# Warm-up products of 512 columns in place of 128, in a fused attention and gated-MLP block

## The chip, the cores and the metric

The kernel runs on one core of one Trainium2 chip. The metric is device time in microseconds (us) of one execution. Several runs of a kernel are taken and their median is quoted with the lowest and the highest; one further execution is taken with the hardware profiler on, and all rows of the trace come from that one. The engines are named as the profile names them: PE (TensorE, matrix products; PEld is its loading of weights), DVE (VectorE), ACT (ScalarE), POOL (GpSimd) and SP (SyncE, which here only issues transfers).

## What is computed

The input x has 2048 tokens of 512 features in bf16. It is normalised, and two branches work on the result: attention with 32 heads of 16 features in a sliding window of 256 tokens, and a gated MLP whose gate mixes tokens with a 2048 x 2048 matrix. The output is the sum of x and both branches.

```python
xn = layernorm(x)                                   # 2048 x 512
# branch A
q, k, v = split(xn @ wqkv)                          # 32 heads of 16
p = softmax(mask(q @ k.T / 4))                      # 0 <= i - j < 256
A = (p @ v) @ wo
# branch B
z = gelu(xn @ w_in)                                 # 2048 x 1376
z1, z2 = z[:, :688], layernorm(z[:, 688:])
B = (z1 * (w_sp @ z2 + b_sp[:, None])) @ w_out
out = x + A + B
```

## The kernel before, in words

Tokens are cut into 16 blocks of 128, one partition per token of the block. The program is one long order written out by hand: three strings, STAGE1, STAGE2 and STAGE3 (lines 68 to 172), hold short commands such as `t,0,v`, and `run` (line 616) executes them one after another by a table of functions (line 607). No scheduler reorders anything; every engine works through its own instructions in the order of these strings, and waits where a tile that it needs isn't ready.

STAGE1 prepares x and computes gelu(xn @ w_in). For each block, `a` takes mean and variance on DVE (lines 263 to 266). The first three blocks go a quicker way than the others: `B` only subtracts the mean on DVE into xc (line 275), `t` transposes the block on PE in four products with the identity (line 284), `T` copies the transposed halves from PSUM into xcT on ACT (line 290), and the scale by 1/sqrt(variance) is applied later. The gate `z` multiplies a block by w_in (lines 304 to 315): per chunk of 128 features one product of 512 and one of 176 columns, four chunks, into one of three PSUM tiles, za, zb and zo. `y` applies gelu on ACT (line 322). From block 3 on the input is normalised in full before it is transposed. STAGE2 computes the projections, attention scores, exponentials and weighted sums together with the token mixing, and STAGE3 the last output projections.

Ahead of STAGE1 the function that holds the kernel issues the loads of x and w_in on the queues of SP and ACT (lines 666 to 677), lets POOL build the identity matrix `ident` (line 680), and calls `table(0)`, which makes ACT load its function table, and `warm(WARM)`. The function `warm(n)` (lines 647 to 651) issues n products on PE of the identity with the identity. Their results go into the PSUM tile zo and are never read; the gate of block 2, the first real writer of zo, overwrites them. WARM is 29 (line 33). The command `W,5` in the first line of STAGE1 (line 69) calls `warm` again with five, between the transposes of block 0 (`t,0,v`) and the copy of them (`T,0,v,A`):

```python
WARM = 29
...
a,0 B,0 a,1 t,0,v W,5 T,0,v,A B,1 A,0,2 z,0,1,a,0,1 t,1,w T,1,w,A a,2 z,0,1,a,1,2 z,1,1,b,0,1
```

So the order on PE at the start is: 29 warm-up products, four transposes of block 0, five warm-up products, the first half of the gate of block 0 (two chunks), four transposes of block 1, the second half of that gate, and so on.

## Time and profile before

| | us |
|---|---|
| median of 3 runs | 259.92 |
| lowest and highest | 258.59 and 260.62 |
| profiled execution, its own time | 258.91 |
| its span, first to last instruction | 257.1 |
| PE busy | 248.5 |
| DVE busy | 186.0 |
| ACT busy | 181.0 |
| POOL busy | 90.9 |

The span is the time between the first and the last instruction of the program on the core; the 1.8 us beside it lie around it. Busy times are of each engine by itself, and they overlap. In the rows below, a name such as L649 is a line of the kernel; `zo<-ident` means that the instruction reads ident and writes zo; `x29` is the number of instructions that a row gathers. The ends of products on PE are modelled, since products overlap in the array: the distance between two starts tells more than the duration of one.

### The profile page before, as it was taken

The numbers are of one execution on the slowest core, as the hardware profiler recorded it, in microseconds if no ns is written. First come the engines' busy times: TensorE is split into PE (matmuls) and PEld (weight loads), VectorE is DVE, ScalarE is ACT, GpSimd is POOL, SyncE is SP. The second block draws the span as 40 slices with busy tenths as digits, with TensorE's granted clock in tenths as the row PEclk, the third lists the DMA queues.
The fourth block names the chain that finished last, engine by engine and source line by source line (L and its number), as shares of the span: only waits on it lengthen the run. The fifth ranks groups of instructions, "written<-read, shape, count | busy, mean of one in ns | idle before, by whom it ended". The sixth has DMA issues, their size and how long they took to land. (4 is left out here: it accounts for less than half of the span.)

```text
span 257.1 us, 9010 instructions
## 1 busy us (share of the span) xinstructions
PE 248.5 (97%) x3880; PEld 137.1 (53%) x3916; DVE 186.0 (72%) x410; ACT 181.0 (70%) x142; POOL 90.9 (35%) x170
## 2 busy tenths in 40 slices
PE   7999999999999999999999999999999999999994
PEld 6565555433456555555555655655656544444541
DVE  4887877888797686778684776857877577667763
ACT  3686476899978687777868777776777786767400
POOL 7524110430015176017197055505545142511120
PEclk9999999999999999999999999999999999999999
DMA  7995743289404897749669476997755532764433
GB/s 237 362 247 98 118 82 83 61 134 234 96 3 95 102 145 144 129 98 170 116 122 165 105 101 118 123 161 128 156 123 96 94 74 84 112 128 116 115 102 102
DMA packets 69847, 32.65 MB, mean 127 GB/s; under 512 B 60800, under 2 KB 66912, under 8 KB 69808
## 3 DMA queue, kind: packets, MB, share of 16 engines
q1 hardware_dynamic: 64288, 21.19, 44.9%
q0 software_dynamic: 4576, 9.71, 17.6%
q10 hardware_dynamic: 944, 1.19, 1.3%
q8 instruction: 30, 0.49, 0.9%
q14 instruction: 9, 0.07, 0.1%
HBM read 8.41 MB, written 2.10 MB: 41 GB/s over the span
## 5 line engine op out<-in xcount | busy, mean ns | idle before, releaser
L443 ACT ACTIVATE E<-sS 128x2048 bf16<-128x2048 f32 x76 | 142.6, 1877 | 41.9 <-PE sS L429 40.8
L551 PE MATMUL w<-z,wspT 128*128 128x344 bf16 x512 | 92.6, 310 | 0.7 <-DVE z1u L558 0.2
L551 PEld LDWEIGHTS <-wspT 128*128 128x128 bf16 x512 | 46.9, 98 | 31.5 <-issue 5.9
L387 POOL DMA_DIRECT2D kbd<-kz x48 | 29.5, 622 | 59.8 <-DVE kz L379 57.7
L366 POOL DMA_DIRECT2D q<-qs x54 | 28.0, 527 | 30.5 <-DVE qs L355 23.1
L452 DVE TENSOR_TENSOR E<-E,mask 128x1024 bf16<-128x1024 bf16 x52 | 34.7, 676 | 4.3 <-ACT E L443 4.3
L339 PE MATMUL w<-xnT,wqkv 128*128 128x512 bf16 x106 | 35.7, 380 | 0.7 <-issue 0.3
L429 PE MATMUL sS<-q,kbd 32*128 32x320 bf16 (+4 forms) x816 | 30.4, 244 | 0.5 <-ACT E L443 0.2
L558 DVE SCALAR_TENSOR_TENSOR z1u<-w,b_all,z1u 128x344 bf16<-128x344 f32 x32 | 18.2, 568 | 16.3 <-PE w L551 16.2
L518 DVE STREAM_TRANSPOSE a<-oP 128x512 f32<-128x512 f32 x32 | 22.7, 709 | 4.7 <-PE oP L510 4.6
L309 PEld LDWEIGHTS <-xnT 128*128 128x128 bf16 x208 | 18.3, 98 | 12.4
L510 PE MATMUL oP<-E,v_all 64*17 64x256 bf16 (+3 forms) x1920 | 24.7, 230 | 0.0
L510 PEld LDWEIGHTS <-v_all 64*17 64x17 bf16 x1920 | 20.2, 85 | 8.4 <-issue 8.1
L429 PEld LDWEIGHTS <-kbd 32*128 32x128 bf16 x816 | 12.3, 92 | 22.3 <-issue 19.9
L580 PE MATMUL w<-w_out_sb,z1u 128*128 128x512 bf16 x67 | 19.1, 380 | 0.7 <-issue 0.3
L574 POOL DMA_DIRECT2D x_ch<-in_A_x_dram x16 | 8.8, 552 | 27.8 <-DVE out_sb L594 23.5
L339 PEld LDWEIGHTS <-wqkv 128*128 128x128 bf16 x128 | 12.1, 98 | 9.7 <-issue 1.2
L327 DVE BATCH_NORM_STATS2 st<-z 128x6 f32<-128x344 bf16 x32 | 14.4, 493 | 2.7 <-ACT z L322 2.7
L394 PE MATMUL w<-wqkv,xnT 128*128 128x512 bf16 x63 | 16.2, 379 | 0.0
L531 DVE STREAM_TRANSPOSE oT<-b 128x256 bf16<-128x256 bf16 x32 | 14.3, 445 | 1.1
L379 DVE CAST kz<-w 128x256 bf16<-128x256 f32 x26 | 9.8, 418 | 6.8 <-PE w L339 5.3
L580 PEld LDWEIGHTS <-z1u 128*128 128x128 bf16 x96 | 8.6, 97 | 10.2 <-issue 1.2
(90 smaller groups left out, 248.4 us busy)
## 6 DMA issues: line engine op xcount, KB each, us to landing
kbd<-kz POOLq DMA_DIRECT2D x48, 64.0 KB, 3.4
q<-qs POOLq DMA_DIRECT2D x36, 64.0 KB, 3.1
x_ch<-in_A_x_dram POOLq DMA_DIRECT2D x16, 128.0 KB, 3.8
out_dram<-out_sb SPq DMA_DIRECT2D x15, 128.0 KB, 1.9
wqkv<-in_A_wqkv_dram SPq DMA_DIRECT2D x1, 1536.0 KB, 12.0
xs<-in_A_x_dram SPq DMA_DIRECT2D x2, 512.0 KB, 7.2
kbd<-kz SPq DMA_DIRECT2D x16, 64.0 KB, 2.2
q<-qs SPq DMA_DIRECT2D x14, 64.0 KB, 2.0
```

The costliest lines, as they stand in the source:

```text
L309: nc.tensor.matmul(zp[:, lo:hi], lhsT=xcT[:, n, c, :] if n < NCEN else xnT[:, c, n * P : (n + 1) * P], rhs=w_in_sb[:, c, f0 + lo : f0 + hi ...
L339: nc.tensor.matmul(banks[bank], lhsT=wqkv[:, c, col : col + P], rhs=xnT[:, c, tok : tok + 512], start=(c == 0), stop=(c == NDC - 1),)
L366: eng.dma_start(out=q2[h : P : 2, e, c : c + w], in_=t[64 * e : 64 * e + 64, src0 + at : src0 + at + w],)
L387: eng.dma_start(out=kbd[h : P : 2, slot : slot + 4, e, :], in_=t[64 * e : 64 * e + 64, h, :].rearrange("p (k m) -> p k m", k=4),)
L429: nc.tensor.matmul(s_bank(s)[:, off + o : off + o + w], lhsT=kbd[32 * s : 32 * s + 32, slot, ee, :], rhs=q2[32 * s : 32 * s + 32, ee, c : ...
L443: nc.scalar.activation(out=dst, in_=src, func=ACT.Exp, scale=SM_SCALE)
L452: nc.vector.tensor_tensor(out=reg, in0=reg, in1=mask[:].rearrange("p a m -> p (a m)").unsqueeze(1).to_broadcast([P, 8, 128]), op=ALU.mult,)
L510: nc.tensor.matmul(skip_group_check=True, **args)
L518: nc.vector.transpose(out=a32[:].rearrange("p e c r -> p (e c r)"), in_=oP[i % 2][:])
L551: nc.tensor.matmul(banks[bank][:, 0:FQ], lhsT=w[:, c, :], rhs=z2[:, c, half * FQ : (half + 1) * FQ], start=(c == 0), stop=(c == NB - 1),)
L558: nc.vector.scalar_tensor_tensor(out=u, in0=banks[bank][:, 0:FQ], scalar=b_all[:, n : n + 1], in1=u, op0=ALU.add, op1=ALU.mult,)
L580: nc.tensor.matmul(banks[bank], lhsT=uT[:, c, :], rhs=w_out_sb[:, c, :], start=(c == 0), stop=False)
```

## The change

The products of `warm` get four times as many columns: the moving operand is the identity read four times over, by a repeated dimension of its access pattern, and the output is a whole row of 512 float32 columns of zo instead of the first 128. Their number falls from 29 to six ahead of STAGE1 and from five to one within it. In columns that is 3712 and 640 before, 3072 and 512 after. Nothing else is changed.

```diff
-WARM = 29
+WARM = 6
...
-a,0 B,0 a,1 t,0,v W,5 T,0,v,A B,1 A,0,2 z,0,1,a,0,1 t,1,w T,1,w,A a,2 z,0,1,a,1,2 z,1,1,b,0,1
+a,0 B,0 a,1 t,0,v W,1 T,0,v,A B,1 A,0,2 z,0,1,a,0,1 t,1,w T,1,w,A a,2 z,0,1,a,1,2 z,1,1,b,0,1
...
     def warm(n):
         for _ in range(n):
             nc.tensor.matmul(
-                zrot["o"][:, 0:P], lhsT=ident[:], rhs=ident[:], start=True, stop=True
+                zrot["o"][:, 0:512], lhsT=ident[:],
+                rhs=ident[:].unsqueeze(1).to_broadcast([P, 4, P]), start=True, stop=True,
             )
```

## The prediction, made before the changed kernel was run

> **What bounds the kernel now.** I read the page first: which engine fills the span, and at which clock. The rows are busy time, the 40 slices of TensorE (PE) and those of its granted clock.

> ```profile
> span 257.1 us, 9010 instructions
> ...
> PE 248.5 (97%) x3880; PEld 137.1 (53%) x3916; DVE 186.0 (72%) x410; ACT 181.0 (70%) x142; POOL 90.9 (35%) x170
> ...
> PE   7999999999999999999999999999999999999994
> ...
> PEclk9999999999999999999999999999999999999999
> ```

> PE is busy from the first slice to the last, so time lost on PE early in the kernel is lost for good unless PE waits somewhere and can make it up. The second view is the busy time of each engine in stretches that I chose; in each the second number is its length, the next PE's busy time, and the third from the end the granted clock.

> ```profile
> core 0: us, PE busy (x) PEld busy (x) DVE busy (x) ACT busy (x) POOL busy (x), PEclk, DMA share, GB/s
> 1.42:2.00 0.58, 0.58 (x6) 0.58 (x7) 0.00 (x0) 0.00 (x0) 0.53 (x4) 1.00 0.37 19
> ...
> 5.00:5.50 0.50, 0.50 (x9) 0.44 (x9) 0.48 (x1) 0.12 (x1) 0.00 (x0) 1.00 1.07 380
> ```

> ```profile
> 4.94:8.69 3.75, 3.46 (x32) 2.22 (x34) 3.17 (x8) 2.51 (x7) 1.19 (x3) 1.00 1.07 373
> 8.69:48.00 39.31, 39.05 (x266) 23.14 (x270) 31.25 (x88) 25.91 (x41) 9.50 (x20) 1.00 0.64 147
> ...
> 58.00:231.00 173.00, 171.02 (x3138) 94.50 (x3162) 125.09 (x261) 133.91 (x81) 66.99 (x120) 1.00 0.68 120
> ```

> From 8.69 to 48 us PE has 0.26 us of idle time, from 58 to 231 us 2.0 us: a delay that PE carries past 8.69 us reaches the end nearly whole. Before that, 0.29 us of 3.75 is idle. The granted clock reads 1.00 even where the warm-up products run, and there it can't be believed, as the next view shows: the line of those products, with the shortest, middle and longest duration of one in ns.

> ```profile
> L649 PEld LDWEIGHTS <-ident x34: 97/151/151, 1.4 to 5.3; 128*128 128x128 bf16 x34
> L649 PE MATMUL zo<-ident x34: 219/314/314, 1.4 to 5.4; 128*128 128x128 bf16 x34
> its engine sat idle before it (us, times) until:
>   POOL mhalf L681: 1.4, 1
> ```

> The same instruction takes 314 ns early and 219 ns late. Third view, the timeline of the opening: start, length of the run of equal instructions, engine, line, how many, and in brackets what ended the idle time.

> ```profile
> 1.42 3.27 PE L649 MATMUL zo<-ident 128*128 128x128 bf16 x29 [1.42 <-POOL mhalf L681]
> ...
> 3.48 0.69 DVE L265 BATCH_NORM_STATS2 st<-xs 128x6 f32<-128x512 bf16 x1 [2.39 <-DMA xs<-in_A_x_dram]
> ...
> 4.43 0.45 DVE L275 TENSOR_SCALAR xc<-xs,mvx 128x512 bf16<-128x512 bf16 x1
> ...
> 4.94 0.40 PE L284 MATMUL w<-ident,xc 128*128 128x128 bf16 x4 [0.25 <-DVE xc L275]
> ...
> 5.18 0.44 PE L649 MATMUL zo<-ident 128*128 128x128 bf16 x5
> 5.38 0.65 ACT L290 COPY xcT<-w 128x256 bf16<-128x256 bf16 x2 [1.60 <-PE w L284]
> ...
> 5.80 0.76 PE L309 MATMUL za<-w_in_sb,xcT 128*128 128x512 bf16 x4 [0.18 <-ACT xcT L290]
> ...
> 6.40 0.39 PE L284 MATMUL w<-ident,xc 128*128 128x128 bf16 x4
> ...
> 6.62 0.75 PE L309 MATMUL za<-w_in_sb,xcT 128*128 128x512 bf16 x4
> ...
> 6.82 0.65 ACT L290 COPY xcT<-w 128x256 bf16<-128x256 bf16 x2 [0.80 <-PE w L284]
> ...
> 7.47 0.53 PE L309 MATMUL zb<-w_in_sb,xcT 128*128 128x176 bf16 x3
> ...
> 8.69 1.34 PE L309 MATMUL zo<-w_in_sb,xcT 128*128 128x512 bf16 x8
> ```

> And the last warm-up product of the first group alone:

> ```profile
> 4.38 0.31 PE L649 MATMUL zo<-ident 128*128 128x128 bf16 x1
> ```

> The 29 products start (3.27 - 0.31)/28 = 0.106 us apart, the five later ones (0.44 - 0.22)/4 = 0.055 us apart: half the clock against the full one. The last product that starts at 4.38 is still slow (0.31); the transposes at 4.94 are fast ((0.40 - 0.22)/3 = 0.06). So the full clock comes between 4.38 and 4.94 us, some 3.0 to 3.5 us after PE's first product, and it comes just in time: no product of the real work runs slow here. What the real work waits for is its data: x lands (3.48), VectorE (DVE) computes statistics and centres (4.43), PE transposes at 4.94, ScalarE (ACT) copies at 5.38, and the gate starts at 5.80, released by ACT.

> **The change, part by part.** It takes 27 pairs of weight load and product from PE (34 become seven); no other engine and no queue gets or loses an instruction.

> *First group.* A slow product of 512 columns has no row. Per column, 0.106 us for 128 gives 0.42 us for 512; at the full clock it would be half, 0.21. The stretch is the slow one, so I take 0.42. Six then stream for 6 x 0.42 = 2.5 us, from 1.42 to 3.95, in place of 29 x 0.106 = 3.1 us, from 1.42 to 4.49. Directly this is worth nothing: PE waits for DVE until 4.94 in either case. The repeated reading of the identity as a moving operand has no row either; it would begin to delay the transposes only from (4.94 - 1.42)/6 = 0.59 us a product, and the same 512 columns at twice 0.42 would cost 1.6 us. The plain 0.42 is nearest, since the columns lie in the same 256 bytes of each partition.

> *Second group.* Five products of 0.055 us become one of 0.21 us, between the transposes and 5.80. The gate waits there for ACT's copy, and that copy starts at 5.38 while the five are still running, so it waits for the transposes alone. Worth nothing at the full clock.

> *The wide output.* 512 columns of zo are written in place of 128. The next writer of zo is the gate at 8.69, on the same engine and in order: no wait, nothing.

> *What the warm-up leaves behind.* This is the one term that can count. Before, PE streams 3.1 us, has a hole of 4.94 - 4.49 = 0.45 us and goes on. After, it streams 2.5 us and has a hole of 4.94 - 3.95 = 0.99 us. The trace of before shows that 3.0 to 3.5 us from the first product sufficed with that hole; it can't show whether 2.5 us do. One end is nothing: the clock still comes by 4.94. The other end is that PE goes on slow for another such stretch of about 3 us, to 8.0. Worked out by hand from the rows, slow columns at 0.106/128 us: the four transposes 4.94 to 5.37, the wide filler to 5.79; ACT's copies start at 5.37 + 0.2 and the gate at 6.0. Half a gate tile is 0.60 us at the full clock (5.80 to 6.40), so 1.19 slow: to 7.19; transposes to 7.62; the second half runs 0.38 us slow until 8.0 and 0.41 fast, to 8.41. The second tile's copies start at 7.62 + 0.2 = 7.82 instead of 6.82, so the next gate, at 7.47 before, starts at 8.5: 1.0 us late, and from 8.69 on PE has no idle time to win that back. A switch halfway, at 6.5: gate's first half 6.0 to 6.85 instead of 6.40, and all that follows 0.45 us late. So the price is 0 to 1.0, by where the switch falls.

> Which end? The runs of before spread from 258.59 to 260.62, by 2.0 us, although one program runs in all; a switch that falls now before, now after the first real product would spread runs by about that much. That is an inference, but it says that the margin is thin already, and the change makes it thinner by 0.54 us of streaming. I take the middle, 0.45.

> [...]

> **Sum.** 0 + 0 + 0 + 0.45 us, on the profiled execution's 258.91 (span 257.1 and 1.8 around it): 259.4. The median of the runs of before is 259.92, 1.0 above that execution; the forecast is set against the median, 259.92 + 0.45 = 260.4.

> **Rivals.**
> *A: nothing is lost.* The clock comes by 4.94 all the same, since PE needs to be busy for only part of a stretch. For it: in before PE also had holes and was idle up to 1.42. Against it: only one instance in the trace. Time: 259.9.
> *C: slower by over 1%.* PE stays slow through a second stretch as well, to about 11.4, because between 4.94 and 8 it still waits for ACT and DVE and is not seen as busy enough. By the rows: gate halves at 1.19 and transposes at 0.43, one after another from 6.0, give 7.19, 7.62, 8.81, 10.00, 10.43, and the fourth half ends at 11.5, where the third tile's gate began at 8.69: 2.8 us, 262.7. It decides once the switch comes later than about 11. For it: the hole of 0.99 us and ACT's wait on either side of it; against it: slow products fill their waits, PE would be idle for some 0.3 us of those 3.
> [...]
> *F: faster.* Unbroken streams of 512 columns, with one weight load in place of four, count for more, and executions that lose time in before lose none. Time: near the fastest run shown, 258.6 to 258.9. It decides if the weight loads break the stream; against it, twice the 0.055 us of the full clock is 0.11, so the slow products already run without a break between them.

> **How the numbers follow.** A late switch of up to one stretch (0.45, 260.4): 0.42. A, 259.9: 0.38. C, 262.7: 0.12. F, 258.7: 0.08. The likeliest is the first; its own range is 259.9 to 260.9. The range for 8 in 10 takes in A and the runs' own spread below, 258.6, and goes toward C without reaching it, 262.4. What a measurement of this kernel can tell from no change is about 1%, 2.6 us. Faster by that much needs more than F: 0.03. Slower by that much is C and little else: 0.13. Within 1%: 0.84.

> **What will show it.** Right, if after's L649 shows seven products, the first six about 0.42 us apart, ending near 4.0 to 4.2, with PE idle until DVE releases the transposes at 4.94; if the transposes, or the first gate products, last as long as slow ones do (a transpose 314 ns and not 219); and if the gate on zo starts later than 8.69 by what the total loses. A is right if the transposes last 219 ns at 4.94 and zo starts at 8.69. C is right if gate products are still slow at 9 us. The forecast is wrong as a whole if the loss appears behind 8.69, if six wide products last beyond 4.94, or if the start of the gate moves while every product of the real work is fast.

## The result, and the profile after

| | before | after |
|---|---|---|
| median, us | 259.94 (22 runs) | 261.31 (22 runs) |
| ratio, 95% interval | | 1.0053 [1.0036, 1.0071] |
| profiled execution, us | 258.91 | 261.11 |
| its span, us | 257.1 | 259.4 |

The change makes the kernel slower by half a per cent, 1.4 us. The forecast was 260.4 with a range from 258.6 to 262.4, and 84% for "within 1%"; the median lies inside, on the side that was forecast, but the loss is three times the 0.45 us of the sum. Runs that lie more than 1.5% above the fastest of their kernel are left out of the ratio; before has one such run (286.73), after two (264.59 and 264.9), with which the ratio of the means would be 1.0065.

First the page of after. Its clock row is all nines, as before.

```profile
span 259.4 us, 8992 instructions
...
PE 252.4 (97%) x3889; PEld 135.5 (52%) x3889; DVE 186.1 (72%) x410; ACT 181.0 (70%) x142; POOL 90.8 (35%) x170
```

PE is busy 3.9 us longer with 27 products less to do. Part of that is records that are missing in the trace of before (3916 weight loads are recorded there, but 3880 products; here 3889 of each), but part must be slower products. The line of the warm-up products says how they ran, and the timeline of the opening (start, length, engine, line) what came of them.

```profile
L649 PE MATMUL zo<-ident x7: 608/634/634, 1.4 to 5.3; 128*128 128x512 bf16 x7
```

```profile
1.42 2.74 PE L649 MATMUL zo<-ident 128*128 128x512 bf16 x6 [1.42 <-POOL mhalf L682]
...
4.94 0.61 PE L284 MATMUL w<-ident,xc 128*128 128x128 bf16 x4 [0.78 <-DVE xc L275]
...
5.34 0.63 PE L649 MATMUL zo<-ident 128*128 128x512 bf16 x1
...
6.02 1.33 PE L309 MATMUL za<-w_in_sb,xcT 128*128 128x512 bf16 x4
...
7.14 0.63 PE L284 MATMUL w<-ident,xc 128*128 128x128 bf16 x4
...
8.71 0.86 PE L309 MATMUL zb<-w_in_sb,xcT 128*128 128x512 bf16 x4
...
9.41 0.39 PE L284 MATMUL w<-ident,xc 128*128 128x128 bf16 x4
...
10.26 1.34 PE L309 MATMUL zo<-w_in_sb,xcT 128*128 128x512 bf16 x8
```

The six wide products start (2.74 - 0.63)/5 = 0.42 us apart, as worked out. The seventh lasts as long as they do: the clock is still half. The transposes of block 0 take 0.61 us instead of 0.40, the first half of the gate 1.33 instead of 0.76, and the transposes at 7.14 take 0.63 where those at 9.41 take 0.39. So the full clock comes between 8.71 and 9.41, inside the run of 0.86 us. The trace also holds records of the granted clock, which begin with this switch: they put it at 8.94 us here and at 4.59 in before. The gate on zo starts at 10.26 instead of 8.69: 1.57 us late. That is less than the 2.3 us by which the spans differ. The rest shows in the waits of PE (what waited for what: us in total, times, longest):

```profile
PE zo L649 <- POOL mhalf L682: 1.4, 1, 1.4
PE w L551 <- issue: 1.0, 1, 1.0
PE w L284 <- DVE xc L275: 0.8, 1, 0.8
```

The second row is new: PE stood still for 1.0 us ahead of a product of the token mixing (L551), once, and "issue" means that the profile shows nothing that it waited for. The timeline of after finds it at 168.71, and at the same place of the program before runs through:

```profile
166.57 0.76 PE L510 MATMUL oP<-E,v_all 64*17 64x64 bf16 x64
167.26 0.47 PE L551 MATMUL w<-z,wspT 128*128 128x344 bf16 x2
168.71 0.60 PE L551 MATMUL w<-z,wspT 128*128 128x344 bf16 x3 [0.98 <-issue]
```

```profile
165.00 0.76 PE L510 MATMUL oP<-E,v_all 64*17 64x64 bf16 x64
165.69 0.90 PE L551 MATMUL w<-z,wspT 128*128 128x344 bf16 x5
```

No number in the prediction has anything to do with that place, 160 us behind the change. The experiments had to say whether both losses belong to the change, and what each costs.

### The profile page after: what moved, and what is told of

Same layout as the page of the kernel before. It is cut to its first block, busy times and chain, and to the rows that moved or that the text cites. A ratio compares the mean times of both kernels' runs of the same rounds, so it can differ in the third digit from the quotient of the medians.

```text
span 259.4 us, 8992 instructions
## 1 busy us (share of the span) xinstructions
PE 252.4 (97%) x3889; PEld 135.5 (52%) x3889; DVE 186.1 (72%) x410; ACT 181.0 (70%) x142; POOL 90.8 (35%) x170
## 3 DMA queue, kind: packets, MB, share of 16 engines
q10 hardware_dynamic: 944, 1.19, 1.3%
HBM read 8.41 MB, written 2.10 MB: 41 GB/s over the span
## 5 line engine op out<-in xcount | busy, mean ns | idle before, releaser
L551 PE MATMUL w<-z,wspT 128*128 128x344 bf16 x512 | 92.8, 310 | 1.0 <-issue 1.0
L551 PEld LDWEIGHTS <-wspT 128*128 128x128 bf16 x512 | 46.9, 98 | 32.6 <-issue 7.1
L339 PE MATMUL w<-xnT,wqkv 128*128 128x512 bf16 x128 | 41.0, 380 | 0.0
L309 PEld LDWEIGHTS <-xnT 128*128 128x128 bf16 x208 | 18.3, 98 | 12.4
L510 PE MATMUL oP<-E,v_all 64*17 64x256 bf16 (+3 forms) x1920 | 24.5, 230 | 0.0
L510 PEld LDWEIGHTS <-v_all 64*17 64x17 bf16 x1920 | 20.1, 85 | 8.3 <-issue 8.1
L586 PE MATMUL w<-wo_sb,oT 128*128 128x512 bf16 x48 | 14.2, 380 | 0.0
```

Of the source, the lines that this page charges most:

```text
L309: nc.tensor.matmul(zp[:, lo:hi], lhsT=xcT[:, n, c, :] if n < NCEN else xnT[:, c, n * P : (n + 1) * P], rhs=w_in_sb[:, c, f0 + lo : f0 + hi ...
L339: nc.tensor.matmul(banks[bank], lhsT=wqkv[:, c, col : col + P], rhs=xnT[:, c, tok : tok + 512], start=(c == 0), stop=(c == NDC - 1),)
L510: nc.tensor.matmul(skip_group_check=True, **args)
L551: nc.tensor.matmul(banks[bank][:, 0:FQ], lhsT=w[:, c, :], rhs=z2[:, c, half * FQ : (half + 1) * FQ], start=(c == 0), stop=(c == NB - 1),)
```

## The experiments

The kernels ran in three sets (an expectation says "call" for one), each on one chip together with the kernel before. All ratios are to the runs of before in the same set.

**First set: how long, which shape, which of the two groups.** Theory G: what counts is the time that PE streams ahead of the data. Rivals: the shape of the products (S), the filler inside STAGE1 (H), plain scatter (P).

Seven wide products:

```diff
-WARM = 6
+WARM = 7
```

> Seven wide products ahead of STAGE1 instead of six, one in it as in the changed kernel. Theory G: what counts is how much of a stretch of some 3 us ahead of the data PE spends streaming; seven wide ones stream 7 x 0.427 = 3.0 us, to 4.4 us, about as long as the 29 narrow ones (3.1 us, to 4.5). G expects the transposes at 4.94 to last 219 ns in the profiled run, the gate on zo at 8.7 us, and a ratio to the kernel before of 0.998 to 1.002. Rival S (shape: wide products with few weight loads count for less than narrow ones): still late, ratio 1.003 to 1.006. Rival H (the filler of one product in place of five is what fails): still 1.003 to 1.007, since the filler is unchanged.

Fewer narrow ones, the 3072 and 512 columns of the changed kernel:

```diff
-WARM = 29
+WARM = 24
-a,0 B,0 a,1 t,0,v W,5 T,0,v,A ...
+a,0 B,0 a,1 t,0,v W,4 T,0,v,A ...
```

> Narrow products of 128 columns as before, but as few columns as in the changed kernel: 24 and four, 3072 and 512 columns. Theory G: they stream 24 x 0.107 = 2.6 us, to 4.0 us, with the same hole before the transposes as six wide ones, so the clock comes late in many executions: ratio 1.003 to 1.007, and if the profiled run is one of them, transposes of 314 ns at 4.94 and the gate on zo at 9.5 to 10.5 us. Rival S: narrow products count as before, ratio 0.998 to 1.002. Rival H (filler): four products of 128 are nearly the five of before, ratio 0.999 to 1.002.

Six wide ones ahead of STAGE1 and the old filler in it (an edit of the kernel before):

```diff
-WARM = 29
+WARM = 6
...
-    warm(WARM)
+    for _ in range(WARM):
+        nc.tensor.matmul(
+            zrot["o"][:, 0:512], lhsT=ident[:],
+            rhs=ident[:].unsqueeze(1).to_broadcast([P, 4, P]), start=True, stop=True,
+        )
```

> Only the first group is changed: six wide products ahead of STAGE1, and the five narrow ones within it as before. Theory G: the first group decides, ratio 1.003 to 1.007 as for the whole change. Rival H: the filler was what cost the time, ratio 0.998 to 1.002, and fast transposes of block 1 in the profiled run.

Eight wide products:

```diff
-WARM = 6
+WARM = 8
```

> Eight wide products ahead of STAGE1: they stream 3.4 us, to 4.8 us, and leave a hole of 0.1 us before the transposes. Theory G: more streaming than before (3.1 us), so fewer late executions: ratio 0.995 to 1.001, transposes of 219 ns at 4.94, gate on zo at 8.7. Rival S: 1.003 to 1.006. Rival P (the clock comes at a time that the kernel doesn't influence, and the difference found is scatter): ratio 1.000 for all four kernels of this call, within 0.2%, with late and early profiled runs mixed over them.

Measured: seven wide 1.0028 [0.9999, 1.0057], 24 narrow 1.0005 [0.9986, 1.0024], six wide with the old filler 1.0077 [1.0045, 1.0109], eight wide 1.0033 [1.0006, 1.0059]. H falls: with the old filler the loss is all there, and P falls with it. G has it wrong twice in the times: seven and eight wide products stream as long as before or longer and still seem to lose time, 24 narrow ones stream as short as after and lose nothing that shows. It misses in the openings too. Behind seven and behind eight wide products the four transposes last 0.61 us, the slow time; the clock records put the release at 5.78 us for seven and at 7.06 for eight, and the gate on zo starts at 8.91 and 9.40. Only for the 24 narrow ones is the opening what G said, slow transposes, release at 10.54 and zo at 11.00, though their ratio shows no loss:

```profile
4.95 0.61 PE L284 MATMUL w<-ident,xc 128*128 128x128 bf16 x4 [0.78 <-DVE xc L275]
...
10.29 0.87 PE L309 MATMUL zb<-w_in_sb,xcT 128*128 128x512 bf16 x4
```

The ratios by themselves look like S. But the traces show something else. All three wide kernels have a stall of PE near 168 us, and the narrow one has none. Here are the places in six wide ones with the old filler, in eight wide, and in seven wide:

```profile
166.69 0.75 PE L510 MATMUL oP<-E,v_all 64*17 64x64 bf16 x62
169.18 0.20 PE L510 MATMUL oP<-E,v_all 64*17 64x64 bf16 x2 [1.74 <-issue]
```

```profile
165.70 0.76 PE L510 MATMUL oP<-E,v_all 64*17 64x64 bf16 x64
167.96 0.89 PE L551 MATMUL w<-z,wspT 128*128 128x344 bf16 x5 [1.51 <-DVE oT L531]
```

```profile
165.89 0.32 PE L551 MATMUL w<-z,wspT 128*128 128x344 bf16 x1
168.53 0.74 PE L551 MATMUL w<-z,wspT 128*128 128x344 bf16 x4 [2.32 <-issue]
```

Count the instructions. These programs have 46, 50 and 52 PE instructions fewer than before, and the changed kernel 54 (a weight load and a product for each pair). The stall stands two products ahead of the end of the 64, exactly at their end, one product behind it, and in after two behind it. Two pairs, four instructions; one pair, two instructions; and so on: the stall is tied to a fixed number of instructions counted from the start of the program, not to a piece of work. (The releaser named in the second fence is only the nearest event; in the others it is "issue".) The page of before lists a queue of the kind "instruction":

```profile
q8 instruction: 30, 0.49, 0.9%
```

That row of the page of before has 30 packets and 0.49 MB, 16 KB each; with 3916 pairs, or 7832 loads and products, it comes to some 63 bytes for each. That the queue is PE's is inferred from this and from the times. The trace has the packets one by one: in before two of them start at 153.1 and 161.2 us; in after the corresponding ones at 156.1 and 165.8. There PE runs dry at 167.73, 0.45 us behind the landing of the second packet, and starts again at 168.71, 1.43 us behind it. In each of the six profiled executions of this study that have the stall, PE starts again 1.4 to 1.8 us after that packet has landed, although the packet's start moves from 165.1 to 167.3 us. Hence theory O, offset: fewer instructions move the boundaries of the fetched blocks, and one of them now falls where the fetch comes too late.

**Second set: the instruction count, both ways.** Tiny pairs (a weight load of 64 x 17 and a product of one column) bring the count back to that of before without much streaming:

```diff
+    def pad(n):
+        for i in range(n):
+            s = i % 4
+            nc.tensor.matmul(
+                zrot["o"][32 * s : 32 * s + DH + 1, 0:1], lhsT=ident[0:64, 0 : DH + 1],
+                rhs=ident[0:64, 0:1], start=True, stop=True,
+            )
...
     warm(WARM)
+    pad(27)
```

> The changed kernel, with 27 tiny pairs of weight load (64 x 17) and product of one column added behind the six wide ones, in the hole before the transposes, so that PE's instruction count is that of the kernel before again (34 pairs at the start). In all four kernels with wide products the trace has one stall of PE without a releaser at 168 to 169 us (0.98 to 2.32 us), at the same place of PE's instruction stream, and none in the two with narrow products. Theory O (offset): removing about 50 instructions moves the boundaries of the blocks in which PE's instructions are fetched (16 KB each), and one then falls where PE eats instructions fastest. O expects the stall gone and a ratio of 1.000 to 1.003, what is left being the late clock, as with 24 narrow products (1.0005). Rival S (the wide shape delays the clock): ratio 1.004 to 1.007 as before, since the shape is the same.

The same with WARM = 7 and pad(26):

> Seven wide products and 26 tiny pairs behind them: as many columns as before (3584 for 3712) and the instruction count of the kernel before. Theory O: no stall at 168 us, ratio 0.998 to 1.002 (1.0028 without the pairs). Rival S: 1.002 to 1.005, as without the pairs.

And the reverse, the warm-up of before untouched and 27 pairs taken out at another place, in visit 2 of L510:

```diff
+    skipped = []
...
+                skipped.append(i == 2 and not args["start"] and not args["stop"])
+                if skipped[-1] and sum(skipped) <= 27:
+                    continue
                 nc.tensor.matmul(skip_group_check=True, **args)
```

> The kernel before, its 29 and five narrow products untouched, with 27 pairs left out of the sums of weights and values in visit 2 (some 0.3 us of PE's work; so part of the attention of one block is not computed). PE has 54 instructions fewer from there on, exactly as in the changed kernel. Theory O: the stall of 1 to 2.3 us at 167 to 169 us appears although the warm-up is that of before, ratio 1.002 to 1.007. Rival S and the clock theory: no stall, ratio 0.998 to 1.000.

Last, WARM = 0, no `W,5`, and pad(34):

> No warm-up products at all, 34 tiny pairs in their place so that the instruction count stays: the price of the clock alone. Theory G (the clock comes only after some 3 us of streaming): real work runs slow from 4.94 to somewhere between 8 and 12 us in every execution; by the working in the prediction (1.0 us for a switch at 8.0, 2.8 for one at 11.4) and the late executions that before has as well, ratio 1.003 to 1.009, zo's gate at 9.7 to 11.6 us. If a late clock costs nothing in the end, ratio 0.999 to 1.002.

Measured: six wide with pairs 1.0048 [1.0022, 1.0074], seven wide with pairs 0.9998 [0.9980, 1.0016], narrow with 27 pairs less 1.0031 [1.0005, 1.0056], no warm-up 1.0054 [1.0035, 1.0073]. Without a warm-up the release is at 10.50 and zo's gate starts at 10.98, as expected; with seven wide ones they are at 5.70 and 9.61, where PE waits for data as well. The third is the clearest: its warm-up is that of before, its transposes at 4.94 are fast (0.40 us for the four), and its timeline shows the stall of the changed kernel at the changed kernel's place, behind the second product of L551 (here L556):

```profile
165.23 0.76 PE L515 MATMUL oP<-E,v_all 64*17 64x64 bf16 x64
165.92 0.47 PE L556 MATMUL w<-z,wspT 128*128 128x344 bf16 x2
167.77 0.60 PE L556 MATMUL w<-z,wspT 128*128 128x344 bf16 x3 [1.38 <-issue]
```

With the pairs added, six wide products run through there:

```profile
167.20 0.76 PE L510 MATMUL oP<-E,v_all 64*17 64x64 bf16 x64
167.89 0.90 PE L551 MATMUL w<-z,wspT 128*128 128x344 bf16 x5
```

O is shown in both directions: the stall comes and goes with the count alone. Seven wide products at the right count cost nothing that shows, so the wide shape as such costs nothing either, and the time that seven and eight lost was the stall's. What O seems to have wrong is the rest: six wide products without the stall were expected at 1.003 at most, and measure 1.0048, though the interval reaches down to 1.0022. By the middles the late clock is the larger part; the intervals do not separate the two.

**Third set: columns or shape for the clock, and the longest warm-up that fits.** 24 and four narrow products again, with pad(6):

> 24 and four narrow products (2.6 us of streaming) with six tiny pairs behind the first group, so that the instruction count is that of the kernel before. Open after the last call: 24 and four narrow products gave 1.0005, six and one wide ones with the count restored 1.0048, though both stream 3072 columns in 2.56 us. Theory C (columns alone decide about the clock): this kernel and six wide ones with 27 pairs agree, both 1.002 to 1.005. Rival S (narrow products, with a weight load for each 128 columns, count for more): this kernel 0.998 to 1.002, the wide one 1.003 to 1.007.

Six and one wide ones with pad(27) beside them:

> The six and one wide products with 27 tiny pairs once more, beside the narrow kernel of this call. Theory C: 1.002 to 1.005, the same as the narrow one. Rival S: 1.003 to 1.007, at least 0.003 above the narrow one. Either way no stall at 168 us.

The changed kernel itself:

> The changed kernel itself once more, for its profile and for its distance to the kernel with 27 pairs in the same call. Offset theory: the stall at 167 to 169 us is there again, 1 to 2.3 us long, and the ratio is 1.004 to 1.009, above the kernel with the 27 pairs by 0.001 to 0.004. If the stall of the first profile was chance, no stall and the same ratio as with the pairs.

Eight wide ones, with pad(25) ahead of them on a tile that DVE sets first:

```diff
+    first = pers.tile([P, 32], BF, name="first")
+    nc.vector.memset(first[:], 1.0)
...
-WARM = 6
+WARM = 8
...
+    pad(25)
     warm(WARM)
```

Here `pad` reads `first` in place of the identity.

> The longest warm-up that fits: 25 tiny pairs on a tile of its own that DVE sets first (so that PE need not wait for the identity), then eight wide products to 4.8 us, one in STAGE1, instruction count as before. Gate and offset theory: no stall, fewer late executions than before: ratio 0.996 to 1.001. Rival S: 1.002 to 1.005, as eight wide ones without the pairs gave 1.0033.

Measured: narrow 1.0035 [1.0012, 1.0058], wide 1.0040 [1.0018, 1.0063], the changed kernel 1.0064 [1.0038, 1.0089], eight wide 1.0002 [0.9978, 1.0026]. At the same count and the same columns, narrow and wide agree as far as the intervals tell, and the 0.003 by which S sets them apart is not seen. That leaves the 1.0005 of 24 narrow products in the first set beside 1.0035 here. The two programs differ by six tiny pairs, their intervals overlap from 1.0012 to 1.0024, and the clock comes early in some executions and late in others, so twelve runs can fall either way; by the ratios alone S is not excluded. The eight wide products, expected as low as 0.996, gain nothing over before; their release is at 7.21 and zo's gate at 9.48. No kernel of the study is shown to be faster than before.

How much chance there is in the clock, two executions of one program show (six wide, 27 pairs): the profiled run of the second set, then that of the third.

```profile
4.95 0.61 PE L284 MATMUL w<-ident,xc 128*128 128x128 bf16 x4 [0.51 <-DVE xc L275]
```

```profile
4.95 0.40 PE L284 MATMUL w<-ident,xc 128*128 128x128 bf16 x4 [0.52 <-DVE xc L275]
```

In the one the transposes run at half clock and the gate on zo starts at 10.69, in the other at the full clock, and it starts at 8.94. The releases are at 9.79 and 4.93.

An estimate of what decides comes from laying the traces out in windows. In all 14 of them the time between two switches of the clock is a whole multiple of 3.413 us (252.59 us in before are 74 of them, 249.17 in after 73, and 163.84 are 48), so windows of this length are counted back from the release; that they run ahead of it as well was not shown. Taking 0.107 us for 128 columns from each recorded start, PE streamed 81 to 100% of the window that ends in the release, in one case 72% with tiny pairs in another 10%; of no earlier window did it stream more than 73%, or 79% with tiny pairs. The shape makes no difference in this: windows of 66 to 72% with 24 narrow products and of 64 to 73% with six wide ones were both passed over. With the transposes left out, windows of 61 and 63% would have been enough and one of 68% not, so transposes seem to count. Where the windows lie differs from execution to execution: the releases of the two above, 9.79 and 4.93, are 4.86 us apart, 1.42 windows. Six wide products stream 2.56 us, 75% of a window, which by itself falls short of the 81% even where one window holds them all. An estimate from these shares for a warm-up that streams on from 1.43 us nearly without a break: it is released at the first end of a window after about 4.2 us, so anywhere up to 7.6, whatever its length. The releases of before, of seven and of eight wide ones (4.51 to 7.21) all lie there, and by this estimate eight do no better than seven.

The changed kernel's stall came again in this set, 2.17 us long at the same place, and it brought a second loss that seven wide products had shown as well. The busy times of the latter in stretches around its stall (start:end, length, PE, then the other engines, the granted clock, third from the end):

```profile
166.20:168.53 2.33, 0.01 (x1) 0.00 (x0) 0.85 (x3) 0.39 (x1) 0.63 (x2) 1.00 1.09 126
168.53:169.60 1.07, 1.07 (x21) 0.55 (x21) 0.00 (x0) 0.00 (x0) 0.00 (x0) 1.00 1.15 277
169.60:173.00 3.40, 3.40 (x15) 1.57 (x12) 0.28 (x1) 1.88 (x1) 0.00 (x0) 0.50 1.18 120
```

Behind 2.3 us without a product the clock falls to half for 3.4 us. The stalls of 0.98 to 1.74 us had no such consequence. In the windows of 3.413 us, PE was busy for 32 and 46% of the two behind which the clock fell, and for 57 to 71% of those with the shorter stalls. One such stretch of half clock takes 0.5 x 3.4 us from some 260, so the mean granted clock of the execution reads 0.993. Of the 76 executions of kernels with 46 to 54 instructions fewer 15 read 0.994 or less; of the other 81 of changed programs and the 95 of before in these three sets none reads below 0.996.

## Why the prediction was right, and where it was not

- *The warm-up products themselves:* right. 0.42 us apart, over long before 4.94, no direct cost; the wide output and the repeated operand cost nothing that shows (seven wide at the right count: 0.9998). At twice 0.42 us the delay worked out there would be 1.5 us and not 1.6 (six of 0.84 from 1.42 end at 6.46); nothing hangs on it.
- *The clock as the one term that can count:* right in kind. Switching late in a part of the executions, losing between 4.94 and the first gate on zo, nothing won back up to there by PE: all seen. Over the eight profiled executions without a stall the span grows by about 0.8 us for each us by which zo's gate starts later (257.1 at 8.69 to 259.6 at 10.98), give or take 0.6, so what is lost there does reach the end in the main. The gate's start at 10.26 agrees with the working: for a switch at 8.0 it gave a loss of 1.0 us, for 11.4 one of 2.8, so for 8.94 some 1.5; measured 1.57.
- *Its size:* the term that was mis-sized. The sum took the middle between the switch at 4.94 and at 8.0, 0.45 us. Six wide products with the old instruction count gave 1.0048 and 1.0040, on average 1.0044, and 0.0044 x 259.6 = 1.1 us; as many columns in narrow products gave 1.0035, and 1.0005 with twelve instructions fewer. The unknown was laid out wrongly: the switch at 8.0 was an estimate from the 3.0 to 3.5 us of before, and in the seven profiled executions with some 2.6 us of streaming the clock came once at 4.93 and six times between 8.49 and 10.54, never between 4.94 and 8.0. Without any warm-up the ratio is 1.0054, 1.4 us; by the intervals six wide products can't be told from none. Whether before has late executions too, as the prediction inferred from its scatter, stays open: the two profiled executions with its warm-up switch at 4.59 and 4.51.
- *"It takes 27 pairs from PE; no other engine and no queue gets or loses an instruction":* the step that failed. It costed the removal of 54 instructions at nothing and overlooked that the instruction stream is itself a transfer (30 packets of 16 KB in the page of before). The stall behind it costs 1.0031 by the kernel with 27 pairs less, which also has some 0.3 us less to do; 1.0028 against 0.9998 with seven wide products, and 1.0033 against 1.0002 with eight, say the same, about 0.8 us. The changed kernel against the one with 27 pairs in the same set, 1.0064 against 1.0040, says 0.6 us. Together with the 1.1 us that makes 1.7 to 1.9 us, or 1.0066 to 1.0073. Measured were 1.0053 [1.0036, 1.0071] and 1.0064 [1.0038, 1.0089]: the sum lies at the upper end of the first interval, in part just above it, and inside the second.
- *Its own signs:* seen are the six products 0.42 us apart, the slow transposes and the late gate on zo. Not met is that zo comes late by what the total loses: 1.57 of 2.3 us in the profiled executions. And the sign for "wrong as a whole", a loss behind 8.69, is met by the 0.98 us at 167.7. So the account of the opening holds and the account of the whole is incomplete. That the median lies in the range all the same is owed to the range's width: the two losses, put at 0.45 us and at nothing, came to 1.4 us.
- *Rivals:* A is true of single executions (the one at 8.94 above), not of the median. C's long second stretch of half clock comes up in single executions without the full price: with 24 narrow products the release at 10.54 made zo's gate 2.3 us late, not 2.8, and that execution took 260.55 and not 262.7. F is not borne out: wide products show no advantage over narrow ones (1.0040 and 1.0035).

On the clock, the half clock of 3.40 us in the fence above fits the multiples of 3.413 us. PE did not have to stream 3.4 us without a break: of the two executions with 2.6 us of streaming and 0.3 of tiny pairs one was released at 4.93, with 0.52 us of idle time just before its transposes.

On the instruction stream, PE waits 0.98 to 2.32 us at this one boundary in six profiled runs; in before, none of its waits for "issue" is longer than 0.2 us. Why that one block comes late stays open. In the six profiled runs with the stall the fetch starts 9.7 to 11.7 us after the one before it, in the eight without 7.4 to 8.5. Transfers are dense there (the column DMA share reads 1.09 from 160 to 168 us in after, and 1.17 in before), and PE goes through 64 of its shortest pairs (L510) in 0.7 us shortly before it. Which of these delays the fetch was not separated. By the count the same boundary lies 25 pairs ahead of the end of the 64 in before, and 19 ahead with 24 narrow products, and there nothing stalls; two pairs ahead of it (46 instructions fewer) it does.

## What to carry to other kernels

What counted of the warm-up here was the time streamed and not the number of products, as far as the intervals tell (2.56 us in 24 narrow products and in six wide ones: 1.0035 and 1.0040), and it bought a better chance of an early clock, not the early clock itself (releases at 4.51 to 7.21 us with 3.0 us or more, at 4.93 to 10.54 with 2.6): 3.0 us of it in wide products lost nothing here against 3.1 us in narrow ones, 2.6 us measured 0.05 to 0.5% slower in four kernels' runs, and none 0.5%. Taking 54 instructions from PE brought a stall of 0.98 to 2.17 us near 168 us, which cost 0.6 to 0.8 us and was gone with the count put back; when time is lost far behind an edit, at a wait that nothing releases, restore the count with cheap instructions and look again before blaming the edit itself. And a stall of PE cost more than its length where it took the clock down with it (here 2.17 and 2.32 us did, 1.74 did not).
